# One POOL task a step: scattered stores, running counts and fold sums each tied behind a step's low parts

## The chip, the cores and the metric

The kernel runs on one core of one Trainium2 chip. The metric is the device time of one execution in microseconds, as a median of several runs. A core has five engines that work side by side from queues of their own: TensorE (PE in the profile; matrix products into PSUM), VectorE (DVE), ScalarE (ACT), GpSimd (POOL; elementwise work and indirect DMAs) and SyncE (SP; DMA issue). [...]

## The reference, cut to what matters

```python
X = np.fft.fft(x, axis=1)              # x: 8 x 3072 x 256
X = np.fft.fft(X, axis=2)
x = X.real.reshape(8 * 3072, 256)      # 24576 tokens
h = x @ w_in                           # 256 -> 2048
g = h * np.clip(h + 3.0, 0.0, 6.0) / 6.0
x = g @ w_out                          # 2048 -> 256
expert_idx = np.argmax(x @ w_gate, axis=1)          # one of 8
gate_w = softmax(x @ w_gate)[expert_idx]
out[mask] = gate_w * (np.maximum(x[mask] @ w1[e], 0.0) @ w2[e])   # for each expert e, 256 -> 1024 -> 256
```

## The kernel before, in words

Numbers are carried as two parts, high and low, and a product of two such numbers is three products (high x high, high x low, low x high).

**First stage.** It runs over 8 images (`b`) and, in each, over 6 chunks of 512 tokens (3 groups `g`, 2 halves `c`): 48 chunks in all. A chunk is 8 steps, one for each 256 of the 2048 hidden columns; `step(s)` writes down the instructions of step `s`, so an image is 48 steps and `s % 8` is the place in a chunk. In a step, TensorE multiplies the spectrum `pq` by two blocks of `w_in` into a PSUM tile `ab` (`mm1`; there are two such tiles), and three steps later (`LAG = 3`) the gated result by `w_out` into four accumulators `acc` (`mm2`; 16 matmuls with the high parts `gh`, 8 with the low parts `gl`). Between them, for the step before, VectorE forms `S` and two halves of `h` from `ab` (which frees the tile), ACT forms `r = relu(h/6 + 1/2)`, VectorE the gate product `r <- min(r, 1) * h` (L506, two a step), ACT the high part `gh` and POOL the low part `gl = r - gh` (L183, two a step). `r`, `gh` and `gl` have four buffers each, which is two steps' worth.

After a chunk's last step ACT moves `acc` to SBUF (`xo`) and halves it into `xp`; then `routing` hands out its stages over the following steps through the table `fill`: `s0` and `s1` on VectorE find each token's expert (`rt_oh` is the one-hot choice, L561), `s2` on POOL forms running counts by expert (one copy, then one add of 128x8 for each of four token tiles, L569 and L572), `s3_mm` and `s3` turn them into row numbers `pi` by a small matmul in a tile like `ab`, and `s4(t)` on POOL stores the rows of token tile `t` at scattered places of `xs` by an indirect DMA (`scat`, L148), four a chunk. `s3` comes at `s % 8 = 2` of the next chunk and `s4(0)` to `s4(3)` in the four steps after it.

Beside this, `plan_folds` spreads the preparation of the next image's transform: VectorE's sums over the loaded rows `R` and over `H`, and POOL's four fold sums for each of four quarters (`H <- R`, L180 and L183). It is used for images 1 to 6; image 0 has a plan of its own, and image 7 prepares nothing. `plan_fft` places the transform's own matmuls at fixed steps of an image. `plan_extra` handles one extra row for each image (frequency 128 of the second axis) in image 7, from step `x0 = 7 * 48 + EXTRA`: `parts`, then the matmuls `exbc`, `exa` and `exo` with their VectorE and ACT work (`bc_ev` holds VectorE's outer product) and a low part `exr` on POOL.

**Second stage.** From about 2140 us the scattered rows are read back by expert, and two matrix products run on each tile of rows.

The order in which an engine executes is not that of the source. A scheduler orders each engine's queue from the recorded program; `tc.keep_in_program_order` pins an instruction to the recorded order, and a dependency without a semaphore between two instructions of one engine only says that one comes after the other there.

Of the kernel before, what the change touches and what calls it, by code (L numbers as in the profile page):

```python
# [12 lines left out]
BF16 = mybir.dt.bfloat16  # L13
# [9 lines left out]
P = 128  # L23
# [23 lines left out]
BUFS = dict(h=2, r=4, gh=4, gl=4)  # L47
EXTRA = 23
LATE = (0, 0, 1, 1, 2, 3, 3, 4, 5, 5, 6, 6, 7, 7, 8, 8, 8, 9)
# [25 lines left out]
def tile_fft_moe(ctx, tc, xr, xf, xcoef, w_in, w_out, w_gate, w1, w2, tabs, fm, misc, tri, sgn8, dstc, maskc, out):  # L75
# [69 lines left out]
    dve, act, pool, pe, sp = nc.vector, nc.scalar, nc.gpsimd, nc.tensor, nc.sync  # L145

    def scat(group, **kw):
        i = pool.indirect_dma_start(oob_is_err=False, **kw)  # L148
        tc.declare_no_dep(i.ins, group=group, reason="distinct rows")
        tc.add_to_no_dep_group(group, i.ins)  # L150
# [15 lines left out]
    def pinned(i):  # L166
        if hold.get("fold"):
            tc.keep_in_program_order(i)

    def in_order(f):  # L170
        hold["fold"] = True
        f()
        hold["fold"] = False
# [5 lines left out]
    def add(eng, o, a, b):  # L179
        pinned(eng.tensor_tensor(out=o, in0=a, in1=b, op=ALU.add))  # L180

# [358 lines left out]
    def routing(xo, xp, t0, nt, mask, tagn, wait=RKW):  # L540
# [24 lines left out]

        def s2():
            st["oc"] = oc = sm("rt_oc", [P, 4, NE], BF16)
            oh = st["oh"]
            pool.tensor_copy(oc[:, 0], cnt)  # L569
            for t in range(nt):  # L570
                o = oc[:, t + 1] if t + 1 < nt else cnt
                pool.tensor_tensor(out=o, in0=oc[:, t], in1=oh[:, t], op=ALU.add)  # L572

# [26 lines left out]

        return [("f", s0), ("f", s1), ("f", s2)] + [("f", lambda: None)] * wait + [("p", s3_mm, s3)] + [("f", lambda t=t: s4(t)) for t in range(nt)]

    if True:
# [93 lines left out]
        def plan_folds(b):  # L697
# [6 lines left out]
            for n in range(24, 28):  # L704
                at[n] = max(at[n], FFT_AT[2][1] + 1 + (n - 24) // 2)
            assert at[32] < FFT_AT[0][0] and at[39] < FFT_AT[1][0] + 6 * STEPS
            for o, hf, n in ((oa, 0, 0), (oa, 1, 4), (ob, 0, 8), (ob, 1, 18)):
                fill[u0 + at[n] - AHEAD].insert(0, o[9 * hf])
                for f in o[9 * hf + 5:9 * hf + 9]:
                    fill[u0 + at[n + 3] + 1].append(lambda f=f: in_order(f))  # L710
            for f, n in zip(seq, at):
# [209 lines left out]
        def step(s):  # L921
# [22 lines left out]
            if 0 < s <= NS:  # L944
# [9 lines left out]
                for n in range(2):  # L954
                    sub(pool, gl[n], g[n], gh[n])
                hold[("g", s - 1)] = (gh, gl)
# [319 lines left out]
```

## Time and profile before

| | |
|---|---|
| median of 3 runs | 3331.14 us (3330.49 to 3333.17) |
| the profiled execution's own time | 3328.47 us |
| its span, first to last instruction | 3326.5 us |
| busy: TensorE, VectorE, ACT, POOL | 3061.1, 2603.8, 1808.6, 2290.0 us |
| the `gl` of POOL (L183), 768 | 1128.5 us |
| the gate products of VectorE (L506), 768 | 730.3 us |
| mean granted clock of TensorE | 0.973 of full speed |

The span is shorter than the execution's time by 1.97 us of start and end. The busy times are sums over stages with different limits: the share of an engine in the whole says little on what a stage waits for, so stretches and timelines are read below.

### The profile page before, as it was taken

Reading aid. Unit: us, or ns where it says so; the run is one execution under the profiler, and the core shown is the slowest. Engines: PE = TensorE matmul, PEld = TensorE weight load, DVE = VectorE, ACT = ScalarE, POOL = GpSimd, SP = SyncE. Lnnn points to the kernel's source line nnn. Section 1 sums busy time; section 2 is a strip of 40 time slices with the busy share of each in tenths; the row PEclk is TensorE's granted clock in tenths of the full one; section 3 lists DMA queues with packets and bytes.
Section 4 is the critical chain, followed back from the end, with each engine's and each line's share of the span. In section 5 each row is a group of like instructions: output and inputs, shape, how many; then the busy total and the mean of one; then the engine's idle time right before and its main releaser. Section 6 shows DMA issues by size and latency. Waiting matters only on the chain. (4 is left out here: it accounts for less than half of the span.)

```text
span 3326.5 us, 61143 instructions
## 1 busy us (share of the span) xinstructions
PE 3061.1 (92%) x22747; PEld 2927.8 (88%) x22747; DVE 2603.8 (78%) x4258; ACT 1808.6 (54%) x3020; POOL 2290.0 (69%) x1781
## 2 busy tenths in 40 slices
PE   5888889889999989989989999999999999999998
PEld 5888889889899889989989998888888888898887
DVE  8999999999999998999999997855555555555553
ACT  4556556555555555556556665544454454454453
POOL 5577776876876866876876665666666666666664
PEclk9999999999999999999999999999999999999999
DMA  5110100100100100100000002075555555555560
GB/s 194 39 35 28 38 25 13 40 23 14 43 25 14 42 25 14 37 30 14 33 14 16 14 14 52 21 206 150 145 167 145 144 155 154 148 146 154 148 171 29
DMA packets 246830, 242.77 MB, mean 73 GB/s; under 512 B 148379, under 2 KB 209660, under 8 KB 246528
## 3 DMA queue, kind: packets, MB, share of 16 engines
q1 hardware_dynamic: 225280, 184.33, 19.7%
q0 software_dynamic: 21248, 54.49, 4.5%
q8 instruction: 181, 2.97, 0.4%
q14 instruction: 121, 0.99, 0.1%
HBM read 159.71 MB, written 54.04 MB: 64 GB/s over the span
## 5 line engine op out<-in xcount | busy, mean ns | idle before, releaser
L183 POOL TENSOR_TENSOR gl<-r,gh 128x512 fp32r<-128x512 f32 x768 | 1128.5, 1493 | 461.4 <-ACT gh L953 251.2
L511 PE MATMUL acc<-WO,gh 128*128 128x264 f32 x6144 | 851.6, 293 | 12.7 <-ACT xo L530 11.6
L511 PEld LDWEIGHTS acc<-WO,gh 128*128 128x128 f32 x6144 | 814.0, 198 | 13.9 <-ACT xo L530 12.0
L506 DVE SCALAR_TENSOR_TENSOR r<-r,h 128x512 f32<-128x512 f32 x768 | 730.3, 976 | 51.6 <-ACT r L499 49.4
L953 ACT ACTIVATE gh<-r 128x512 fp32r<-128x512 f32 x768 | 473.7, 630 | 528.7 <-DVE r L506 390.0
L499 ACT ACTIVATE r<-h,half 128x512 f32<-128x512 f32 x768 | 523.9, 720 | 272.6 <-DVE h L183 207.0
L164 PE MATMUL ab<-pq,WA 128*128 128x256 f32 x2304 | 417.7, 291 | 151.0 <-DVE rt_mc L549 72.2
L987 DVE SCALAR_TENSOR_TENSOR WB<-hp,WA 128x512 fp32r<-128x512 f32 (+1 forms) x472 | 278.7, 606 | 304.2 <-ACT WA L986 300.0
L164 PEld LDWEIGHTS ab<-pq,WA 128*128 128x128 f32 x2304 | 337.4, 193 | 161.0 <-issue 137.6
L511 PE MATMUL acc<-WO,gl 128*128 128x264 f32 x3072 | 440.8, 285 | 4.1 <-POOL gl L183 4.1
L164 PE MATMUL ab<-pq,WB 128*128 128x256 f32 x2304 | 414.8, 290 | 0.0
L511 PEld LDWEIGHTS acc<-WO,gl 128*128 128x128 f32 x3072 | 401.1, 189 | 6.3 <-POOL gl L183 6.2
L188 DVE SCALAR_TENSOR_TENSOR S<-pb,w,ab 128x256 f32<-128x256 f32 x768 | 333.9, 472 | 52.1 <-PE ab L164 51.2
L986 ACT ACTIVATE WA<-hp 128x512 fp32r<-128x512 f32 (+1 forms) x472 | 241.4, 531 | 195.5 <-PE hp L164 194.7
L164 PEld LDWEIGHTS ab<-pq,WB 128*128 128x128 f32 x2304 | 342.5, 196 | 0.0
L148 POOL DMA_INDIRECT out_dram<-yo,dst x200 | 217.8, 1089 | 156.0 <-DVE yo L1087 118.5
L164 PE MATMUL hp<-xTb,TB 128*128 128x512 f32 (+1 forms) x1344 | 277.2, 364 | 13.6 <-DVE WB L987 13.6
L164 PE MATMUL op<-W2b,WA 128*128 128x256 f32 x1536 | 277.8, 283 | 0.0
L164 PE MATMUL hp<-xTa,W1b 128*128 128x512 f32 (+1 forms) x1392 | 275.6, 357 | 1.9 <-DVE WB L987 1.9
L164 PEld LDWEIGHTS hp<-xTb,TB 128*128 128x128 f32 x1344 | 225.7, 188 | 57.8 <-DVE WB L987 15.3
L148 POOL DMA_INDIRECT xs_dram<-xp,pic x192 | 215.1, 1120 | 84.8 <-issue 28.4
L1087 DVE TENSOR_SCALAR yo<-op,gd 128x256 f32<-128x256 f32 x200 | 95.4, 478 | 219.6 <-PE op L164 217.8
(268 smaller groups left out, 5208.6 us busy)
## 6 DMA issues: line engine op xcount, KB each, us to landing
w1a<-in_w_dram SPq DMA_DIRECT2D x29, 1024.0 KB, 5.0
w1b<-in_w_dram SPq DMA_DIRECT2D x29, 1024.0 KB, 4.9
w2b<-in_w_dram SPq DMA_DIRECT2D x58, 512.0 KB, 4.0
R<-in_xr_dram SPq DMA_DIRECT2D x32, 774.0 KB, 4.2
w2a<-in_w_dram SPq DMA_DIRECT2D x29, 768.0 KB, 4.9
w2d<-in_w_dram SPq DMA_DIRECT2D x28, 256.0 KB, 4.3
raw<-in_w_in_dram SPq DMA_DIRECT2D x8, 512.0 KB, 4.1
rawo<-in_w_out_dram SPq DMA_DIRECT2D x8, 512.0 KB, 3.4
```

The lines of the kernel that those rows point to most:

```text
L148: i = pool.indirect_dma_start(oob_is_err=False, **kw)
L164: pe.matmul(dst, l, r, start=(n == 0), stop=(n == len(terms) - 1))
L183: i = eng.tensor_tensor(out=o, in0=a, in1=b, op=ALU.subtract)
L188: pinned(dve.scalar_tensor_tensor(out=o, in0=a, scalar=s, in1=b, op0=ALU.mult, op1=ALU.add))
L499: act.activation(r, h, AF.Relu, bias=half, scale=1.0 / 6.0)
L506: dve.scalar_tensor_tensor(out=g, in0=r, scalar=1.0, in1=h, op0=ALU.min, op1=ALU.mult)
L511: pe.matmul(acc[t][:, 0:GW], lhs, wo(w, f0 + i), start=st, stop=sp_)
L953: act.activation(gh[n], g[n], AF.Copy)
L986: act.activation(hi, ps, AF.Relu)
L987: dve.scalar_tensor_tensor(out=lo, in0=ps, scalar=0.0, in1=hi, op0=ALU.max, op1=ALU.subtract)
L1087: dve.tensor_scalar(yo[:, j], ps[:, 0:D], t["gd"][:, j, 0:1], None, op0=ALU.mult)
```

## The change

A helper `behind(i)` is new: it adds an order without a semaphore, so that instruction `i` comes after the latest `gl` that has been recorded (`hold["gl"]`, set in `step`). It is applied to each scattered store into `xs`, to each instruction of the running counts, and in `plan_folds` to POOL's fold sums. `s2` becomes `s2(t)`, one add a step over four steps, where all stood in one step before. The four fold sums of a quarter are put into four steps, one each, in place of one step for all; they are no longer pinned to the recorded order. The extra row starts two steps later (`EXTRA` 25).

```diff
-EXTRA = 23
+EXTRA = 25
...
+    def behind(i):
+        tc.add_manual_dep(i.ins, hold["gl"].ins.name, mybir.DependencyInfo(mybir.DependencyClass.NoSync, mybir.DependencyReason.DATA),
+                          reason="one a step")
+
     def scat(group, **kw):
         i = pool.indirect_dma_start(oob_is_err=False, **kw)
+        if group == "xs":
+            behind(i)
...
     def add(eng, o, a, b):
-        pinned(eng.tensor_tensor(out=o, in0=a, in1=b, op=ALU.add))
+        i = eng.tensor_tensor(out=o, in0=a, in1=b, op=ALU.add)
+        pinned(i)
+        return i
...
-        def s2():
-            st["oc"] = oc = sm("rt_oc", [P, 4, NE], BF16)
-            oh = st["oh"]
-            pool.tensor_copy(oc[:, 0], cnt)
-            for t in range(nt):
-                o = oc[:, t + 1] if t + 1 < nt else cnt
-                pool.tensor_tensor(out=o, in0=oc[:, t], in1=oh[:, t], op=ALU.add)
+
+        def s2(t):
+            if t == 0:
+                st["oc"] = sm("rt_oc", [P, 4, NE], BF16)
+                behind(pool.tensor_copy(st["oc"][:, 0], cnt))
+            oc = st["oc"]
+            o = oc[:, t + 1] if t + 1 < nt else cnt
+            behind(pool.tensor_tensor(out=o, in0=oc[:, t], in1=st["oh"][:, t], op=ALU.add))
...
-        return [("f", s0), ("f", s1), ("f", s2)] + [("f", lambda: None)] * wait + [("p", s3_mm, s3)] + [("f", lambda t=t: s4(t)) for t in range(nt)]
+        return [("f", s0), ("f", s1)] + [("f", lambda t=t: s2(t) if t < nt else None) for t in range(wait + 1)] + [("p", s3_mm, s3)] + [("f", lambda t=t: s4(t)) for t in range(nt)]
...
-                for f in o[9 * hf + 5:9 * hf + 9]:
-                    fill[u0 + at[n + 3] + 1].append(lambda f=f: in_order(f))
+                for k, f in enumerate(o[9 * hf + 5:9 * hf + 9]):
+                    fill[u0 + at[n + 3] + 1 + k].append(lambda f=f: behind(f()))
...
                 for n in range(2):
-                    sub(pool, gl[n], g[n], gh[n])
+                    hold["gl"] = sub(pool, gl[n], g[n], gh[n])
```

On POOL, at the end of a chunk of image 4 that has no fold sums near it (steps 218 to 222), the queue of the kernel before reads so; the number behind `gl` is the step that recorded it, and `x3` is three instructions alike:

```order
L183 TENSOR_TENSOR gl218_0_15747<-r218_0_15743,gh218_0_15745 128x512
L183 TENSOR_TENSOR gl218_1_15748<-r218_1_15744,gh218_1_15746 128x512
L569 COPY rt_occ26_15975<-cnt_63 128x8
L148 DMA xs_dram<-xp207_15196,pic25_15767 198656x260 x3
L572 TENSOR_TENSOR rt_occ26_15975<-rt_occ26_15975,rt_ohc26_15910 128x8
L148 DMA xs_dram<-xp207_15196,pic25_15767 198656x260
L572 TENSOR_TENSOR rt_occ26_15975<-rt_occ26_15975,rt_ohc26_15910 128x8 x2
L572 TENSOR_TENSOR cnt_63<-rt_occ26_15975,rt_ohc26_15910 128x8
L183 TENSOR_TENSOR gl219_0_15824<-r219_0_15820,gh219_0_15822 128x512
L183 TENSOR_TENSOR gl219_1_15825<-r219_1_15821,gh219_1_15823 128x512
```

The changed kernel's queue at the same place, on the same engine:

```order
L192 TENSOR_TENSOR gl219_1_15825<-r219_1_15821,gh219_1_15823 128x512
L153 DMA xs_dram<-xp207_15193,pic25_15767 198656x260
L192 TENSOR_TENSOR gl220_0_15892<-r220_0_15888,gh220_0_15890 128x512
L192 TENSOR_TENSOR gl220_1_15893<-r220_1_15889,gh220_1_15891 128x512
L153 DMA xs_dram<-xp207_15193,pic25_15767 198656x260
L192 TENSOR_TENSOR gl221_0_15960<-r221_0_15956,gh221_0_15958 128x512
L192 TENSOR_TENSOR gl221_1_15961<-r221_1_15957,gh221_1_15959 128x512
L153 DMA xs_dram<-xp207_15193,pic25_15767 198656x260
L579 COPY rt_occ26_15975<-cnt_63 128x8
L582 TENSOR_TENSOR rt_occ26_15975<-rt_occ26_15975,rt_ohc26_15910 128x8
L192 TENSOR_TENSOR gl222_0_16026<-r222_0_16022,gh222_0_16024 128x512
L192 TENSOR_TENSOR gl222_1_16027<-r222_1_16023,gh222_1_16025 128x512
```

Nothing stands between the low parts of steps 218 and 219 any more; the stores follow one behind each pair from step 219 on, and the copy and the adds one behind each from step 221 on.

Where POOL's fold sums are near (image 4, steps 196 to 198), the queue before reads on POOL:

```order
L572 TENSOR_TENSOR rt_occ23_14339<-rt_occ23_14339,rt_ohc23_14251 128x8 x3
L572 TENSOR_TENSOR cnt_63<-rt_occ23_14339,rt_ohc23_14251 128x8
L183 TENSOR_TENSOR gl197_0_14315<-r197_0_14311,gh197_0_14313 128x512
L183 TENSOR_TENSOR gl197_1_14316<-r197_1_14312,gh197_1_14314 128x512
L180 TENSOR_TENSOR H5_1_13552<-R5_1_0_13550 128x2x129
L183 TENSOR_TENSOR H5_1_13552<-R5_1_0_13550 128x2x129
L183 TENSOR_TENSOR H5_1_13552<-R5_1_0_13550 128x129
L180 TENSOR_TENSOR H5_1_13552<-R5_1_0_13550 128x129
L183 TENSOR_TENSOR gl198_0_14393<-r198_0_14389,gh198_0_14391 128x512
```

And in the changed kernel:

```order
L192 TENSOR_TENSOR gl197_1_14316<-r197_1_14312,gh197_1_14314 128x512
L187 TENSOR_TENSOR H5_1_13552<-R5_1_0_13550 128x2x129
L153 DMA xs_dram<-xp183_13543,pic22_14107 198656x260
L579 COPY rt_occ23_14336<-cnt_63 128x8
L582 TENSOR_TENSOR rt_occ23_14336<-rt_occ23_14336,rt_ohc23_14251 128x8
L192 TENSOR_TENSOR gl198_0_14387<-r198_0_14383,gh198_0_14385 128x512
L192 TENSOR_TENSOR gl198_1_14388<-r198_1_14384,gh198_1_14386 128x512
L192 TENSOR_TENSOR H5_1_13552<-R5_1_0_13550 128x2x129
L153 DMA xs_dram<-xp183_13543,pic22_14107 198656x260
L582 TENSOR_TENSOR rt_occ23_14336<-rt_occ23_14336,rt_ohc23_14251 128x8
L192 TENSOR_TENSOR gl199_0_14451<-r199_0_14447,gh199_0_14449 128x512
```

One fold sum, one store and one add now stand between two steps' low parts, in several steps on end, where four fold sums stood in a row.

Around the extra row (image 7), POOL's queue before:

```order
L183 TENSOR_TENSOR gl362_1_25716<-r362_1_25712,gh362_1_25714 128x512
L148 DMA xs_dram<-xp351_25115,pic43_25735 198656x260 x4
L183 TENSOR_TENSOR gl363_0_25799<-r363_0_25795,gh363_0_25797 128x512
L183 TENSOR_TENSOR gl363_1_25800<-r363_1_25796,gh363_1_25798 128x512
L183 TENSOR_TENSOR exr_25422<-exf_25423,exr_25422 128x128
```

And in the changed kernel:

```order
L192 TENSOR_TENSOR gl364_0_25873<-r364_0_25869,gh364_0_25871 128x512
L192 TENSOR_TENSOR gl364_1_25874<-r364_1_25870,gh364_1_25872 128x512
L153 DMA xs_dram<-xp351_25115,pic43_25684 198656x260
L192 TENSOR_TENSOR exr_25540<-exf_25541,exr_25540 128x128
L192 TENSOR_TENSOR gl365_0_25945<-r365_0_25941,gh365_0_25943 128x512
```

The low part `exr` now follows one store and the low parts of step 364, where it followed four stores and those of step 363.

## Rows read from the trace of the kernel before

**Rows 1.** Windows, us busy (x instructions) by engine, TensorE's granted clock, DMA share, GB/s

```profile
300.00:2000.00 1700.00, 1552.31 (x12314) 1529.40 (x12313) 1589.97 (x2657) 1002.29 (x1768) 1258.24 (x1104) 0.96 0.07 25
```

**Rows 2.** Groups, 300 to 2000 us: count, busy us, mean ns, idle before and releasers

```profile
L506 DVE SCALAR_TENSOR_TENSOR r<-r,h 128x512 f32<-128x512 f32 x642 | 605.0, 968 | 47.1 <-ACT r L499 44.9
...
L164 PE MATMUL ab<-pq,WA 128*128 128x256 f32 x1920 | 346.4, 290 | 133.0 <-DVE rt_mc L549 72.2 <-DVE xp L591 28.5 <-DVE rt_sc L590 24.0
...
L561 DVE SCALAR_TENSOR_TENSOR rt_ohc<-rt_ixc,iom 128x32 bf16<-128x32 f32 x40 | 26.7, 667 | 0.0
```

**Rows 3.** Timeline of TensorE, 1250 to 1275 us: start, length, instruction, idle before

```profile
1258.96 0.59 PE L164 MATMUL ab<-pq,WA 128*128 128x256 f32 x3 [2.64 <-DVE rt_mc L549]
...
1260.84 3.26 PE L511 MATMUL acc<-WO,gh 128*128 128x264 f32 x16
...
1264.90 0.52 PE L164 MATMUL ab<-pq,WA 128*128 128x256 f32 x3
...
1266.34 2.10 PE L511 MATMUL acc<-WO,gh 128*128 128x264 f32 x16
...
1269.26 0.52 PE L164 MATMUL ab<-pq,WA 128*128 128x256 f32 x3
```

**Rows 4.** Timeline of POOL, 1256.5 to 1290 us

```profile
1256.90 2.51 POOL L183 TENSOR_TENSOR gl<-r,gh 128x512 fp32r<-128x512 f32 x2 [1.79 <-ACT gh L953]
...
1261.40 0.98 POOL L148 DMA_INDIRECT xs_dram<-xp,pic  x1 [0.30 <-issue]
...
1262.69 1.42 POOL L148 DMA_INDIRECT xs_dram<-xp,pic  x1 [0.30 <-DVE r L506]
...
1266.41 6.23 POOL L183 TENSOR_TENSOR gl<-r,gh 128x512 fp32r<-128x512 f32 x4
...
1283.13 3.00 POOL L183 TENSOR_TENSOR gl<-r,gh 128x512 fp32r<-128x512 f32 x2 [1.79 <-ACT gh L953]
```

**Rows 5.** Timeline of VectorE, 1256.5 to 1290 us

```profile
1258.14 0.68 DVE L180 TENSOR_TENSOR h<-S,ab 128x512 f32<-128x512 f32 x1
...
1261.97 1.29 DVE L506 SCALAR_TENSOR_TENSOR r<-r,h 128x512 f32<-128x512 f32 x2
...
1267.33 2.62 DVE L506 SCALAR_TENSOR_TENSOR r<-r,h 128x512 f32<-128x512 f32 x2
...
1271.40 1.78 DVE L506 SCALAR_TENSOR_TENSOR r<-r,h 128x512 f32<-128x512 f32 x1
...
1283.64 1.33 DVE L180 TENSOR_TENSOR H<-H 128x516 f32<-128x516 f32 x1
```

**Rows 6.** Timeline of ACT, 1260 to 1266 us

```profile
1263.65 1.15 ACT L953 ACTIVATE gh<-r 128x512 fp32r<-128x512 f32 x2 [1.27 <-PE acc L511]
```

**Rows 7.** Timeline of ACT, 1142 to 1150 us

```profile
1145.82 0.72 ACT L499 ACTIVATE r<-h,half 128x512 f32<-128x512 f32 x1 [1.48 <-POOL gl L183]
```

**Rows 8.** Timeline of VectorE, 1152 to 1165 us

```profile
1158.18 3.19 DVE L506 SCALAR_TENSOR_TENSOR r<-r,h 128x512 f32<-128x512 f32 x2 [0.25 <-ACT r L499]
```

**Rows 9.** Timeline of VectorE, 1226 to 1238 us

```profile
1227.02 0.18 DVE L557 SCALAR_TENSOR_TENSOR rt_kc<-rt_dc,iom 128x32 f32<-128x32 f32 x1
...
1228.45 3.06 DVE L561 SCALAR_TENSOR_TENSOR rt_ohc<-rt_ixc,iom 128x32 bf16<-128x32 f32 x1
```

**Rows 10.** Timeline of TensorE, 1226 to 1238 us

```profile
1233.85 0.59 PE L164 MATMUL ab<-pq,WA 128*128 128x256 f32 x3 [2.94 <-DVE xp L591]
```

**Rows 11.** Timeline of POOL, 1343 to 1386 us

```profile
1361.13 13.67 POOL L183 TENSOR_TENSOR gl<-r,gh 128x512 fp32r<-128x512 f32 x8
```

**Rows 12.** Groups of POOL with shapes kept apart, 300 to 2000 us

```profile
L180 POOL TENSOR_TENSOR H<-R 128x258 f32<-128x258 f32 x24 | 25.4, 1057 | 0.0
```

**Rows 13.** Timeline of TensorE, 2004 to 2042 us

```profile
2029.92 7.91 PE L164 MATMUL exo<-WO,exr 128*8 128x264 f32 x46 [4.29 <-POOL exr L183]
```

**Rows 14.** Timeline of POOL, 2017 to 2033 us

```profile
2028.95 0.92 POOL L183 TENSOR_TENSOR exr<-exf,exr 128x128 fp32r<-128x128 f32 x1
```

**Rows 15.** Waits of ACT, 300 to 2000 us: total, times, longest

```profile
ACT r L499 <- POOL gl L183: 36.9, 44, 1.5
```

More of the change, by code (lines that the diff above doesn't have):

```diff
@@ L705, in plan_folds @@
                 at[n] = max(at[n], FFT_AT[2][1] + 1 + (n - 24) // 2)
+            assert at[7] + 4 <= at[12] and at[21] + 4 <= at[28]
             assert at[32] < FFT_AT[0][0] and at[39] < FFT_AT[1][0] + 6 * STEPS
```

## Prediction

> **What bounds the kernel now.** I read the windows first. From 300 to 2000 us, where the Fourier stage and the first expert layer run, VectorE is busy 1590 of 1700 us and TensorE 1552 [rows 1]. So two engines are nearly full, and the question is who makes whom wait. The groups of that stretch answer it: TensorE idles 133 us, all of it ahead of the first matmul of a step, for VectorE to free the PSUM tile `ab`; the names in its row are of whatever VectorE finished last [rows 2]. The same group view shows why VectorE is full. Its gate product (L506, two a step) takes 968 ns on average [rows 2], but 1.29 us for a pair, 0.65 each, where nothing disturbs it [rows 5]. 640 of them at 0.32 us too much are about 205 us.
>
> The timelines of steps 218 to 224 show how the two belong together. TensorE does a step in 4.36 us (1264.90 to 1269.26) until a chunk ends; there the routing takes one of the two `ab` tiles, TensorE waits 2.64 us until VectorE has read the last one (1258.14 + 0.68, and 0.14 later TensorE starts), and the next 16 matmuls take 3.26 us in place of 2.10 [rows 3, 5]. So a chunk lasts as long as VectorE needs from the moment it falls behind to the chunk's end, and only what shortens VectorE there shortens the program.
>
> VectorE's long products stand beside POOL's low parts. The product at 1271.40 takes 1.78 us while `gl` runs [rows 5, 4]: an elementwise POOL operation and a VectorE operation with two inputs in SBUF take turns, each for a whole instruction. A scatter on POOL doesn't do that: the pair at 1261.97 ran beside two scatters in 1.29 us [rows 5, 4].
>
> In steady steps the two engines miss each other: POOL is idle 1.79 us before its pair of `gl` [rows 4], and there VectorE's pair of products fits. What breaks this is the burst after a chunk's end: copy, four scatters and four adds stand on POOL ahead of `gl219`. ACT has the first half of `gh` ready at about 1264.2 [rows 6], POOL starts its four `gl` at 1266.41, 2.1 us late [rows 4], and the next two products of VectorE cost 2.62 us as a pair, the one after them 1.78 [rows 5].
>
> **The change, part by part.** No instruction is added or removed. TensorE's and ACT's orders change around the extra row alone; VectorE's there and by a swap or two an image. POOL's changes throughout, in all chunks; SP's not at all. The expert stage after 2140 us keeps its order.
>
> *Scatters and adds.* `gl219` can start when `gh` is there, 1264.3, and both halves, at 1.25 each [rows 4], are over by 1266.9, before the pair at 1267.33: 1.33 us less on VectorE. The product at 1271.40 may keep its wait (0) or lose it (1.1). The scatters now fill the idle 1.79 us of four later steps. A scatter with its 0.30 us of issue takes 1.3 alone and 1.7 beside products (0.98 and 1.42) [rows 4], so it fits; the copy and an add are some 0.6 more (between the second scatter's end, 1262.69 + 1.42, and 1266.41 [rows 4] stand one scatter of about 1.0 and the four adds, so 0.3 each), and in that step POOL comes 1.7 + 0.6 - 1.79 = 0.5 us late, a little less in the next. Nothing is queued behind on POOL but that step's `gl`, for which VectorE's fold operation waits already (1.33 us at 1283.64 [rows 5]). I give back 0.7 us a chunk for this, and take 1.0 us net, from bounds of 0 and 2.4.
>
> Per image (six chunks) the kinds of chunk differ. Three have a burst alone: two at 1.0, and 0 for the one where a Fourier piece on TensorE lets VectorE catch up in mid-chunk: 2.0. One has four fold sums on POOL shortly before the burst: there the one-hot comparison of 128x32 took 3.06 us while the late `gl` pair ran, and TensorE waited 2.94 us behind it [rows 9, 10]. Undisturbed I put this operation at about 0.2, from the 0.18 us of one of its size [rows 9]; 667 ns is its mean [rows 2]. With `gl` on time it meets at most a fold sum (1.06 [rows 12]): 2.0 less, from bounds of 0 and 2.9. One has fold sums right behind the burst: ACT waited 1.48 us for a buffer of `r` that a late `gl` still read, and a pair of products cost 3.19 instead of 1.29 [rows 7, 8]. Of these 3.4 I take 2.0; below, 0. In the last kind POOL runs eight `gl` without a pause in 13.67 us, 1.71 each where 1.25 would do [rows 11], and fold sums behind them: POOL is full, and spreading full work moves nothing: 0, between -1 and +1. The sum is 6.0 us an image. Six images (1 to 6) are of this kind: 36 us. Image 0 keeps its fold sums in place and image 7 has none; for them I count nothing.
>
> The running counts are read by the routing matmul two or more steps after their last add, and the scattered rows' buffer is wanted again a chunk later; I cost both waits at nothing. If the cover failed, TensorE would wait for a 0.2 us add.
>
> *The extra row, two steps later.* Its low part `exr` now stood behind four scatters and a `gl` pair, ending at 2029.87; TensorE waited 4.29 us for it, and its 46 matmuls then took 7.91 us [rows 13, 14]. In the new order one scatter stands ahead of it, and the chunk's end with its ACT work lies before, not between. The wait goes wholly or to a third, and some of the slow matmuls with it: 5 us, from bounds of 0 and 6.2 (46 at the 0.13 us that 16 in 2.10 [rows 3] make would be 6.0; 4.3 + 1.9).
>
> Sum: 36 + 5 = 41 us. The profiled execution took 3328.47 us; the median shown is 2.67 above, 3331.14. So 3287.5 by the profile, and **3290 us** as a median.
>
> **The rivals.**
> (a) *The phases lock again.* After the burst VectorE and POOL need some four steps to fall back into the steady pattern, and its step with a fold operation (1.79 + 3.00 = 4.79 us [rows 4]) is slower than TensorE's 4.36 whatever came before. Then VectorE reaches the chunk's end hardly earlier: 0.3 us a chunk over 36 chunks, and the extra row: 15 us, 3316. For it: the pattern pulls itself together. Against it: the chunks with fold sums don't reach the pattern in today's trace before they end.
> (b) *More than that.* With shorter waits at the borders the matmuls behind them run in 2.10 in place of 3.26 us, which I have not counted. At the upper bounds alone (3.4 + 2.9 + three at 2.4 + 1 = 14.5 an image, 87 for six, 6.2 for the extra row): 93 us, 3238. Against it: every bound must hold at once.
> (c) *Slower: POOL falls behind for good.* Eight steps an image now hold a fold sum (1.06), a scatter with its issue (1.7), partly a copy and an add (0.6), and the `gl` pair (3.0 [rows 4]): 5.8 to 6.4 us against TensorE's 4.36. Three in a row put POOL 4 to 5 us behind; where that uses up the two steps of slack, ACT waits for `r`, as it does now 44 times for 36.9 us [rows 15]. It decides if that wait comes at three places an image: 1.5 us there and 1.3 of a slowed pair, 50 us over six images, with none of the gain: 3376; with half of it, 3358. For it: the row of eight `gl`. Against it: the same work stands there today in larger lumps.
> (d) *Slower: scatters wait for VectorE's products.* If a scatter beside a pair of products waited out its 1.29 us [rows 5] in place of the 0.44 seen (1.42 less 0.98 [rows 4]), it would take 0.85 more and `gl` come 0.5 us late in four steps of 36 chunks: 72 us back, 3362. The 1.42 speaks against it; it is counted with (c). [...]
> (e) *Nothing*: what a chunk gains in its first steps TensorE's own pace takes: 3331.
>
> **How the numbers follow.** What can be told from no change here is about 0.2%, 6.7 us. Forecast (3265 to 3312): 0.50. (a), 3312 to 3324: 0.15. (b), below 3265: 0.10. (e), within 6.7 us: 0.10. (c) and (d), slower: 0.15. So faster 0.75, same 0.10, slower 0.15. The range runs from the middle of (b), 3250, to the upper side of (e) and the mildest of (c), 3336; outside it I leave 0.07 below and 0.12 above. The forecast's own range is 3265 to 3312.
>
> **What would show it.** Right: after a chunk's end no four scatters in a row on POOL, `gl` within 0.5 us of its `gh`; L506 below 900 ns; the one-hot comparison below 450 ns; ACT's waits for `gl` under 20 us; TensorE's idle time ahead of `ab` between 90 and 110 us in that stretch; no 4.29 us before `exo`. If L506 keeps its 968 ns, (a) or (e). If ACT's waits for `gl` grow past 60 us, (c); scatters of 2 us and more as a rule, (d). The forecast fails if POOL's lateness is not removed but only handed from one step to the next, so that products meet `gl` as often as before.

## The result, and the profile after

The changed kernel takes 3362.68 us (3349.44 to 3369.66, 7 runs) against 3331.12 of the kernel before (7 runs): a ratio of 1.0087 (1.0066 to 1.0108): 31.6 us slower, where 41 us faster was forecast. The profiled execution took 3366.02 us with a span of 3364.2. Within the seven runs the time goes with the mean granted clock of TensorE (3369.66 us at 0.967, 3349.44 at 0.975). The clock alone is not the difference: in the kernel before, run beside the first experiments below, 0.967 goes with 3342.14 us and 0.974 with 3327.08, so at like clock some 22 to 28 us are left (if chips do not differ by as much). Whether the clock is cause or consequence of the rest is not shown. In what follows a *store* is a scatter, one of the 192 indirect DMAs from POOL into `xs`.

The windows and the groups from 300 to 2000 us answer to [rows 1, 2] (the lines moved: L515 is the gate product, L192 the low part, L570 the one-hot choice, L171 `mm1`):

```profile
300.00:2000.00 1700.00, 1528.98 (x12047) 1504.76 (x12046) 1594.52 (x2600) 979.91 (x1729) 1220.69 (x1085) 0.96 0.07 24
```

```profile
L515 DVE SCALAR_TENSOR_TENSOR r<-r,h 128x512 f32<-128x512 f32 x628 | 562.6, 924 | 33.7 <-ACT r L508 32.3
...
L197 DVE SCALAR_TENSOR_TENSOR R<-R 128x516 f32<-128x516 f32 (+1 forms) x47 | 84.2, 1792 | 0.0
L187 DVE TENSOR_TENSOR R<-R 128x516 f32<-128x516 f32 (+1 forms) x47 | 71.9, 1529 | 0.0
L187 DVE TENSOR_TENSOR H<-H 128x516 f32<-128x516 f32 (+1 forms) x36 | 63.2, 1755 | 0.0
...
L570 DVE SCALAR_TENSOR_TENSOR rt_ohc<-rt_ixc,iom 128x32 bf16<-128x32 f32 x39 | 7.1, 182 | 0.0
...
L171 PE MATMUL ab<-pq,WA 128*128 128x256 f32 x1881 | 343.9, 293 | 154.7 <-DVE rt_mc L558 71.8 <-DVE xp L601 37.5 <-DVE h L187 24.4
```

What was forecast for single operations largely came: the gate products fell from 968 to 924 ns, the one-hot choice from 667 to 182. But VectorE is as busy as before and the program gets less far in the stretch. VectorE's fold operations became slower. The same groups of the kernel before:

```profile
L180 DVE TENSOR_TENSOR R<-R 128x516 f32<-128x516 f32 (+1 forms) x47 | 50.9, 1082 | 0.0
L188 DVE SCALAR_TENSOR_TENSOR R<-R 128x516 f32<-128x516 f32 (+1 forms) x47 | 49.7, 1058 | 0.0
L180 DVE TENSOR_TENSOR H<-H 128x516 f32<-128x516 f32 (+1 forms) x36 | 41.3, 1148 | 0.0
```

These three rows alone hold 77 us more (84.2 + 71.9 + 63.2 less 50.9 + 49.7 + 41.3). The timelines of POOL and of VectorE in chunk kind "POOL is full" (image 4) show one of the slow ones:

```profile
1384.14 1.26 POOL L153 DMA_INDIRECT xs_dram<-xp,pic  x1 [0.15 <-PE acc L520]
1385.41 2.56 POOL L192 TENSOR_TENSOR gl<-r,gh 128x512 fp32r<-128x512 f32 x2
1387.92 1.39 POOL L192 TENSOR_TENSOR H<-R 128x258 f32<-128x258 f32 x1
```

```profile
1385.65 3.15 DVE L197 SCALAR_TENSOR_TENSOR R<-R 128x774 f32<-128x774 f32 x1
```

The fold operation comes 0.24 us after the first `gl` has begun. By the prediction it gets its turn at that one's end, some 1 us later, as in [rows 4, 5], where a pair of `gl` with a fold operation between them takes 3.00 us. Here the two `gl` run in 2.56 us without a break and VectorE waits for both. What stands out is that this pair begins right at the end of a store (1384.14 + 1.26); whether that is the reason the experiments have to show.

To count this, each VectorE operation's time above the shortest one of its kind (same operands and shape) was summed over the first stage (from the first low part to the last), by what stood on POOL while it waited: one elementwise operation; two or more that follow a store without a gap (under 60 ns from each to the next; one add of the counts may stand first); two or more elsewhere. These sums are worked out from all instructions of the traces, in us, with the number of operations. They move by up to some 15 us with the limits chosen, the differences between the rows by less:

```
                 stage   one POOL op    2+ behind a store   2+ elsewhere   sum
before            2090   347.7 (518)     49.2 (18)            4.0 ( 4)     401
changed           2124   322.1 (499)    106.1 (51)           11.4 (13)     440
stores            2088   320.6 (483)    100.5 (50)            2.3 ( 2)     424
untied            2130   321.4 (504)    109.6 (34)            9.6 (12)     441
untiedpad         2066   335.0 (549)      0                  27.7 (22)     363
beforepad         2078   343.6 (525)      2.3 ( 2)           17.2 (10)     364
```

The forecast gain is there: 26 us less of waits behind one operation. Against it stand 57 us more behind stores and 7 elsewhere: 39 us more on VectorE, 34 us more of stage. A sum of waits is not yet time, though: the row `stores`, an experiment below, has as much behind stores as the changed kernel and the stage of the kernel before.

### The profile page after: what moved, and what is told of

It reads as the page before. It is cut to its first block, busy times and chain, and to the rows that moved or that the text cites. A ratio compares the mean times of both kernels' runs of the same rounds, so it can differ in the third digit from the quotient of the medians.

```text
span 3364.2 us, 61099 instructions
## 1 busy us (share of the span) xinstructions
PE 3076.3 (91%) x22747; PEld 2943.2 (87%) x22747; DVE 2638.3 (78%) x4258; ACT 1806.9 (54%) x3020; POOL 2285.3 (68%) x1781
## 3 DMA queue, kind: packets, MB, share of 16 engines
q8 instruction: 181, 2.97, 0.4%
## 5 line engine op out<-in xcount | busy, mean ns | idle before, releaser
L192 POOL TENSOR_TENSOR gl<-r,gh 128x512 fp32r<-128x512 f32 x768 | 1076.3, 1422 | 570.2 <-PE acc L520 278.8
L515 DVE SCALAR_TENSOR_TENSOR r<-r,h 128x512 f32<-128x512 f32 x768 | 692.6, 928 | 43.4 <-ACT r L508 41.9
L171 PE MATMUL ab<-pq,WA 128*128 128x256 f32 x2304 | 424.0, 294 | 173.8 <-DVE rt_mc L558 71.8
L171 PEld LDWEIGHTS ab<-pq,WA 128*128 128x128 f32 x2304 | 342.0, 196 | 187.4 <-issue 169.6
L171 PE MATMUL ab<-pq,WB 128*128 128x256 f32 x2304 | 418.2, 292 | 0.0
L171 PEld LDWEIGHTS ab<-pq,WB 128*128 128x128 f32 x2304 | 345.9, 199 | 0.0
L171 PE MATMUL hp<-xTb,TB 128*128 128x512 f32 (+1 forms) x1344 | 277.2, 364 | 13.6 <-DVE WB L998 13.6
L171 PE MATMUL op<-W2b,WA 128*128 128x256 f32 x1536 | 277.9, 283 | 0.0
L171 PE MATMUL hp<-xTa,W1b 128*128 128x512 f32 (+1 forms) x1392 | 275.6, 357 | 1.2 <-DVE WB L998 1.2
L171 PEld LDWEIGHTS hp<-xTb,TB 128*128 128x128 f32 x1344 | 225.9, 188 | 57.6 <-DVE WB L998 15.2
L171 PEld LDWEIGHTS hp<-xTa,W1b 128*128 128x128 f32 x1392 | 227.9, 188 | 41.8 <-DVE WB L998 1.6
```

What stands on the lines that cost most here:

```text
L171: pe.matmul(dst, l, r, start=(n == 0), stop=(n == len(terms) - 1))
L192: i = eng.tensor_tensor(out=o, in0=a, in1=b, op=ALU.subtract)
L515: dve.scalar_tensor_tensor(out=g, in0=r, scalar=1.0, in1=h, op0=ALU.min, op1=ALU.mult)
```

## The experiments

Ratios are to the kernel before, run on the same chip in turn, with 95% intervals. The kernel before took 3331.1 to 3341.5 us from chip to chip (medians), so runs of different chips are compared by their ratios.

**First four: which part, and spacers.** Theories: T1, a VectorE operation loses its turn where two low parts follow a store without a gap (51 operations of the changed kernel, 18 of the kernel before, by the table above; the expectations, which count up to 2000 us and with other limits, have 56 and 16); T2, POOL has too much in each step (rival c); T3, a phase that happens to be bad.

`pads2`: the changed kernel with

```diff
+        if group == "xs":
+            for n in range(2):
+                p = pool.tensor_copy(pad[:, 0:8], pad[:, 8:16])
+                after_of(p, i)
+                i = p
+            hold["pad"] = i
...
```

> The changed kernel with two 128x8 copies on POOL (onto scratch that nobody reads) right behind each of its 192 scattered stores and ahead of the next low part. Three theories stand for the 31.5 us that the change cost. [...] By T1 the copies stand in the place of the pair: losses under 10, VectorE's fold operations (R and H, 256 us for 160 in images 1 to 6, 171 before) back under 190 us, and the time at 3300 to 3330. T2, POOL is late because every step now holds something (rival c of the prediction): 0.4 us more a store makes it worse, 3365 to 3400. T3, the fold operations merely stand at a phase where the pair runs, whatever is ahead of it: losses stay above 40, 3355 to 3375.

3342.23 us, 1.0015 (0.9998 to 1.0032). Waits behind a store fell from 106 to 21 us, and the ratio by 0.7 per cent, less than T1 had forecast: waits behind one operation rose from 322 to 379, with 192 times two copies more on POOL. The ranges of T2 and T3 were missed, so neither is the whole of it.

`lumpfold`, `foldspread`: the fold sums undone, and alone.

```diff
-                for k, f in enumerate(o[9 * hf + 5:9 * hf + 9]):
-                    fill[u0 + at[n + 3] + 1 + k].append(lambda f=f: behind(f()))
+                for f in o[9 * hf + 5:9 * hf + 9]:
+                    fill[u0 + at[n + 3] + 1].append(lambda f=f: in_order(f))
```

> The changed kernel with the four fold sums of a quarter in one lump on POOL again; stores and counts stay one a step. T1 (turn lost behind a store): the stores still stand right ahead of `gl` in busy chunks, so losses stay at 35 or more and the time at 3345 to 3370. T2 (a fold sum in each step overloads POOL): back to 3310 to 3335.

3342.61, 1.0017 (1.0004 to 1.0030): between the two ranges, and below T1's though 89 us of waits behind stores were left.

> The kernel before with its POOL fold sums one a step, each behind that step's low parts; stores, counts and extra row as before. T1: only the burst's last store can stand right ahead of `gl`, so 16 losses or so as before, VectorE's fold operations under 190 us, 3315 to 3335. T2 (a fold sum in each step makes POOL late): 3345 and more.

3330.58, 0.9985 (0.9974 to 0.9996): the fold sums alone cost nothing, so T2 is out for them alone.

`extra25`: the kernel before with `EXTRA = 25`.

> The kernel before with the extra row two steps later and nothing else. The prediction's term of 5 us (bounds 0 and 6.2) gives 3326; a wait that only moves gives 3331.

3330.38, 0.9984 (0.9970 to 0.9999): some 5 us (0.3 to 10), the term of the prediction.

**Next four: other places for the store, and the two engines by themselves.** `mid` puts each store between the two `gl` of the next step, `midlump` also has lumps of fold sums, `scatfirst` puts the store ahead of the fold sum of its step. In the cut from `mid`, `f()` records the store.

```diff
                 for n in range(2):
                     hold["gl"] = sub(pool, gl[n], g[n], gh[n])
+                    if n == 1 and "sc" in hold:
+                        after_of(hold["gl"], hold.pop("sc"))
+                    for f in hold.pop("late", []) if n == 0 else []:
+                        f()
...
```

> The changed kernel with each scattered store between the two `gl` of a step (images 0 to 6) in place of behind the pair; POOL's instructions and their number are the same. T1 (the turn is lost where two low parts follow a store without a gap): only one `gl` now follows a store, and VectorE has the store's own 1 us for itself, so losses of a whole pair under 10, VectorE's fold operations of images 1 to 6 under 200 us (256 in the changed kernel), 3310 to 3340. T2 (POOL has too much in each step): its load is the same, 3350 to 3370.

3388.11, 1.0158 (1.0134 to 1.0182): a miss for both theories. The second `gl` comes a store later, waits behind one operation rise by some 50 us, and over 80 us stay behind stores, now with a fold sum or an add as the second operation.

> The same as the run before it, stores between the two `gl`, and the fold sums of a quarter in one lump again. T1: the some 48 losses of the run with lumps alone (3342.6) go: 3310 to 3335. T2: POOL's load is that of the run with lumps alone, so 3335 to 3350.

3391.52, 1.0162 (1.0138 to 1.0185): the same.

> The changed kernel with one thing turned round: in a step that holds a store and a fold sum, the store comes first, and the fold sum and the add stand between it and the next `gl`. T1: where a fold sum stands there, the pair keeps its handover; where the store is alone, it is lost as before: losses of a whole pair from 56 to some 30, 3340 to 3358. T2: the same work in each step, 3355 to 3370.

3345.93, 1.0023 (1.0010 to 1.0037): the time fell in T1's range, but not for its reason, since some 100 us behind stores stayed. What makes it 0.6 per cent faster than the changed kernel is open.

`byitself`: nothing of the kernel but 480 VectorE additions in a row and a list of POOL work.

```python
    v(60)
    many(12, lambda: gl(2))
    v(60)
    many(8, scat, lambda: gl(2))
    v(60)
    many(8, scat, lambda: gl(4))
    v(60)
    many(8, scat, lambda: copy(1), lambda: gl(2))
    v(60)
    many(8, scat, lambda: copy(2), lambda: gl(2))
...
```

> Not the kernel's work: only POOL and VectorE, and the output is filled with constants. VectorE runs 480 additions of 128x512 in a row; POOL runs 24 subtractions of 128x512, then, eight times each, a scattered store with two subtractions, a store with four, a store with one, two and three 128x8 copies and two subtractions, and a plain DMA from its queue with two. T1: without a store they take turns, an addition in each gap (POOL 1.25 to 1.9 us a subtraction, VectorE some 1.9); behind a store the first two POOL operations run in a row and one addition takes some 3.1 us; with one copy a copy and a subtraction are the two (some 2.1), with two or three copies no loss beyond 1.9; with four subtractions only the first two run in a row. T3: turns throughout, no addition over 2 us. What a plain DMA does is open.

No addition took over 2.2 us, near what T3 has: behind a store VectorE got its turn after the first subtraction. T1 as it stood was not shown outside the kernel.

**The factors one by one.** A new theory, T4: the stores had stood in a hole of POOL.

`untied` takes the tie off the stores, `untiedlump` also undoes the fold sums, `stores` has nothing but the tied stores.

```diff
         i = pool.indirect_dma_start(oob_is_err=False, **kw)
-        if group == "xs":
-            behind(i)
```

> The changed kernel without the tie on the scattered stores alone: they stand again ahead of a chunk's first `gl`, four in a row, while counts and fold sums stay one a step and the extra row late. T4, a new theory: POOL stood idle ahead of that `gl` for some 5.5 us in many chunks, since TensorE and ACT were not yet there; the four stores (4 x 1.3 us) lay in this hole, and the tie moved them into steps that have none, so POOL's idle time ahead of `gl` rose from 353 to 448 us between 300 and 2000 us. By T4 the stores alone cost what was lost and the counts gave a gain: 3300 to 3325. T1 (turns lost behind a store): losses fall from 56 to some 16 to 36, 3315 to 3335. T2 (the sums and counts in every step overload POOL): stays at 3345 and more.

3367.99, 1.0103 (1.0086 to 1.0119): in T2's range, far from those of T4 and T1.

> As the run before it, with the fold sums in lumps too: only the counts one a step, and the late extra row. T4: 3300 to 3325, the counts being what made `gl` late in the kernel before. If the counts are nothing, 3326, the extra row's 5 us alone.

3378.63, 1.0133 (1.0117 to 1.0150): both ranges missed.

> The kernel before with the tie on the scattered stores alone; counts, fold sums and extra row as before. T4 and T1: the whole loss or more, 3350 to 3375, POOL's idle time ahead of `gl` over 420 us from 300 to 2000 us. T2: near the kernel before, 3325 to 3340.

3327.99, 0.9984 (0.9975 to 0.9994): in T2's range, and T1's and T4's were missed. T4 is false, stores tied one a step are no loss. T1 is missed in an instructive way: VectorE did lose its turns, 100 us of them behind stores, and it cost no time. What all slow variants share is the moved *counts*. In the kernel before a copy and four adds stood between the stores and the next `gl`; moved one a step, they leave a store right ahead of it.

`phases`: by themselves again, with additions at all phases.

> Not the kernel's work: only POOL and VectorE, the output filled with constants. VectorE runs an addition with both inputs in SBUF, then one to three with one input in PSUM, of several lengths, so that its two-input additions come at all phases of POOL's work; POOL runs, 24 times each, two subtractions of 128x512 behind one 128x8 copy, behind a scattered store, behind a store and two copies, and behind a plain DMA. T1: an addition that starts inside the first subtraction gets its turn ahead of the second (1.9 us or less from the start of the first) but for the second group, where it waits for both (its end over 2.5 us after the start of the first); a saturated VectorE did not show it, since its addition stood there before the first subtraction. If T1 is wrong, no group differs.

No group differed: a VectorE addition that starts in the first subtraction ends 1.80 to 1.86 us after that one's start, behind a store too (three that start late in it, behind copies, 2.32). By this T1 was wrong, or the kernel had something more.

**What stands behind the last store.** `untiedpad` is `untied` with two copies behind the fourth store of a chunk, in the old place of the counts, and no others.

```diff
+            for n in range(2 if hold.get("lastst") else 0):
+                p = pool.tensor_copy(pad[:, 0:8], pad[:, 8:16])
...
+            hold["lastst"] = t == nt - 1
...
```

> The changed kernel with the stores untied (3368), and two 128x8 copies on POOL, onto scratch that nobody reads, behind the last of a chunk's four stores alone, ahead of the next low part. In the kernel before, the copy and the adds of the counts stood in that place. T1 (a `gl` right behind a store denies VectorE its turns): VectorE's time lost to two and more POOL operations right behind a store falls from 110 us to under 45, and the time to 3325 to 3345. T5, the rival: the counts cost where they now stand, one in each of four steps: no change, 3360 to 3375.

3305.86, 0.9913 (0.9894 to 0.9933): 62 us (1.9 per cent) faster than `untied` by 96 copies of some 0.3 us, and faster than both kernels. That is below T1's range even; T5 is out. Timelines of POOL and VectorE at the same chunk end (steps 218 and 219, image 4), `untied` first:

```profile
1283.59 1.23 POOL L153 DMA_INDIRECT xs_dram<-xp,pic  x1 [0.30 <-issue]
1284.82 2.56 POOL L190 TENSOR_TENSOR gl<-r,gh 128x512 fp32r<-128x512 f32 x2
```

```profile
1285.35 3.19 DVE L513 SCALAR_TENSOR_TENSOR r<-r,h 128x512 f32<-128x512 f32 x2
```

and `untiedpad`:

```profile
1254.97 0.97 POOL L159 DMA_INDIRECT xs_dram<-xp,pic  x1 [0.30 <-issue]
1255.94 0.66 POOL L164 COPY pad<-pad 128x8 bf16<-128x8 bf16 x2
1256.57 2.52 POOL L202 TENSOR_TENSOR gl<-r,gh 128x512 fp32r<-128x512 f32 x2
```

```profile
1258.35 1.89 DVE L525 SCALAR_TENSOR_TENSOR r<-r,h 128x512 f32<-128x512 f32 x2
```

The pair of products costs 1.89 in place of 3.19 us. These rows show more than a turn given back: in `untied` the products start 0.53 us into the pair of `gl` and wait for both, in `untiedpad` 1.78 us into it and wait for the second alone, and there too the pair runs without a break. So part of what the copies bring is that fewer operations meet the pair at all: of the 47 pairs behind them 38 met none that had to wait for their first `gl`, 8 gave the turn. How the 62 us divide between the two is not shown. Some ten steps on, where stores stand between low parts, `untied` has its worst: three `gl` run in a row behind a store, and one product waits for all of them.

```profile
1331.86 3.80 POOL L190 TENSOR_TENSOR gl<-r,gh 128x512 fp32r<-128x512 f32 x3
```

```profile
1331.71 4.50 DVE L513 SCALAR_TENSOR_TENSOR r<-r,h 128x512 f32<-128x512 f32 x1
```

`waits`: as `phases`, but each subtraction takes an input copied for it by ACT, so it waits on a semaphore.

```diff
-            keep(pool.tensor_tensor(out=go, in0=ga, in1=gb, op=ALU.subtract))
...
+            act.activation(hh, gb, AF.Copy)
+            keep(pool.tensor_tensor(out=oo, in0=ga, in1=hh, op=ALU.subtract))
```

> Not the kernel's work: POOL and VectorE by themselves as in the run with all phases, but each subtraction now takes an input that ACT copies for it and waits for it by a semaphore, as `gl` waits for `gh`, with four buffers. Groups of 24: two subtractions behind one copy, behind a store, behind a store and two memsets, behind a store and two copies. T1 needs something that the earlier runs by themselves lacked; if that is the semaphore, additions that start inside the first subtraction end over 2.5 us after its start in the second group and by 1.9 us in the others. If no group differs, the loss in the kernel hangs on more than a store and a wait.

Now the loss is there outside the kernel. Behind a store all 24 additions ended 3.05 to 3.06 us after the first subtraction's start; behind two memsets or two copies the same code gives 1.80 to 1.81 (33 of 37; of those that start late in the first, three ended at 2.3 and one at 3.5; behind one copy without a store one of 13 ended at 2.8). The run has ACT's copies and four buffers beside the semaphores; that it is the semaphores among these is the likeliest reading, but not shown apart. POOL's timeline in the group with a store, and in that with memsets:

```profile
150.98 2.49 POOL L117 TENSOR_TENSOR oo<-ga,hh 128x512 f32<-128x512 f32 x2
153.63 1.26 POOL L133 DMA_INDIRECT xs<-xp,pi  x1 [0.17 <-issue]
154.92 2.49 POOL L117 TENSOR_TENSOR oo<-ga,hh 128x512 f32<-128x512 f32 x2
...
191.02 0.99 POOL L133 DMA_INDIRECT xs<-xp,pi  x1 [0.16 <-issue]
192.02 0.28 POOL L122 MEMSET pad<- 128x8 bf16 x2
192.26 2.94 POOL L117 TENSOR_TENSOR oo<-ga,hh 128x512 f32<-128x512 f32 x2
```

VectorE's additions beside these two (150.98 and 192.26):

```profile
150.99 3.03 DVE L107 TENSOR_TENSOR vo<-va,vb 128x512 f32<-128x512 f32 x1
...
192.43 1.64 DVE L107 TENSOR_TENSOR vo<-va,vb 128x512 f32<-128x512 f32 x1
```

and in the run without semaphores, behind a store:

```profile
101.06 1.26 POOL L124 DMA_INDIRECT xs<-xp,pi  x1 [0.16 <-issue]
102.34 2.97 POOL L113 TENSOR_TENSOR go<-ga,gb 128x512 f32<-128x512 f32 x2
```

2.49 us is two subtractions back to back, 2.94 and 2.97 two with an addition between them.

`nocounts` is the changed kernel with the counts as before; `nocountspad` has two memsets behind each store.

> The changed kernel with the counts alone as before: copy and four adds in one lump, not tied; stores and fold sums one a step, the extra row late. If the parts add up (stores, fold sums and extra row 0.16, 0.15 and 0.16 per cent faster each when alone): 3310 to 3325. If stores and fold sums in the same steps overload POOL (T2): 3335 and more.

3336.65, 1.0007 (0.9993 to 1.0022): without the move of the counts the slowdown is gone, but the three small gains don't add up, and the time is in T2's range. The waits behind stores are not gone: some 100 us, as in the changed kernel.

> The same, with two 128x8 memsets on POOL behind each store. T1: the 100 us that VectorE lost behind stores in the run with tied stores alone fall under 40, 3295 to 3315, if a memset stands in for a copy; if not, as the run before it or some 5 us more.

3335.44, 1.0004 (0.9994 to 1.0015), above T1's range. These two runs differ by the memsets alone and show the turn itself most plainly, and that getting it back need not be worth any time. In `nocounts` 47 `gl` pairs began within 30 ns of a store's end while a VectorE operation waited, and none let it in between; behind the memsets 114 pairs met a waiting operation, and all 114 let it in. One place in both, first `nocounts`:

```profile
1286.70 1.26 POOL L153 DMA_INDIRECT xs_dram<-xp,pic  x1 [0.16 <-issue]
1287.95 2.57 POOL L192 TENSOR_TENSOR gl<-r,gh 128x512 fp32r<-128x512 f32 x2
```

```profile
1288.40 2.42 DVE L184 SCALAR_TENSOR_TENSOR SS0s<-H,SS0s 128x254 fp32r<-128x254 f32 x1
```

and `nocountspad`:

```profile
1292.78 0.30 POOL L166 MEMSET pad<- 128x8 bf16 x2
1293.08 2.72 POOL L204 TENSOR_TENSOR gl<-r,gh 128x512 fp32r<-128x512 f32 x2
```

```profile
1293.23 1.41 DVE L196 SCALAR_TENSOR_TENSOR SS0s<-H,SS0s 128x254 fp32r<-128x254 f32 x1
```

Yet the time is the same: waits behind stores all but went, those behind one operation rose to some 380 us. One store a step with spacers trades one for the other.

**What the counts' move is worth by itself.** `beforepad` is the kernel before with two memsets behind each store, `untiedpadall` is `untied` with the same.

> The kernel before with two 128x8 memsets on POOL behind each store (they take 0.12 us each where measured by themselves). It too lost VectorE's turns behind a store, 18 times, 49 us in all, where no add happened to stand between. If the 26 us of the run with stores untied and copies behind the last store are only these losses cured: 3300 to 3312 here too. If the counts' move, one a step, is a gain by itself, as the prediction had it: some of the 26 us only, 3312 to 3328.

3317.80, 0.9933 (0.9912 to 0.9955). The kernel before took 3341.53 us on this chip, some 10 more than the two ranges were set from; by the ratio, the gain of 0.67 per cent (22 us) is most of the 26 and speaks for the first.

This trace also holds what the runs with a plain DMA by themselves could not show. POOL's queue loads a small table (`sgn`) by a plain DMA once an image, and in six images a `gl` pair follows it within 22 ns, with no memset between. VectorE's operation that needs 0.41 us took 2.52 to 2.90 there, all six times (13 us in all):

```profile
466.04 0.60 POOL L275 DMA_DIRECT2D sgn<-in_sgn_dram  x1
466.66 2.54 POOL L195 TENSOR_TENSOR gl<-r,gh 128x512 fp32r<-128x512 f32 x2
```

```profile
466.96 2.53 DVE L189 SCALAR_TENSOR_TENSOR SC<-H,SC 128x254 fp32r<-128x254 f32 x1
```

> The changed kernel with the stores untied and two 128x8 memsets behind each store in place of two copies behind the last of four. T1: no loss behind a store is left, also not where a store stands between two low parts (6 in the run with copies behind the last): 3295 to 3308. If memsets between the stores lengthen the lump more than they save: 3308 to 3315.

3312.77, 0.9916 (0.9895 to 0.9937). Both intervals hold the other's middle: of the gain of `untiedpad` most is what `beforepad` has too, with the kernel before's own 49 us behind stores cured. Run side by side the two differ by 5 us (3312.11 to 3313.91 against 3316.68 to 3319.93). That is what the move of counts and sums and the late extra row add together, and the extra row's own 5 us would fill it. The six losses that the expectation puts behind stores stand behind `sgn`, and are still here.

## Why the prediction was wrong

*What bounds the kernel*: right in the main. The sum of VectorE's waits beside POOL (401 to 440 us) moved with the stage (2090 to 2124), and the two shortest stages of the table have the two smallest sums. It is not the sum alone: `stores` has 424 us and a stage of 2088, so where a wait falls counts too.

*The step that failed* is the sentence that "an elementwise POOL operation and a VectorE operation with two inputs in SBUF take turns, each for a whole instruction". It holds elsewhere (518 of 540 waiting operations of the kernel before waited for one POOL operation alone), but right behind a store the low parts run on uninterrupted and VectorE waits for both (`waits`: 3.05 us against 1.81; `nocounts` against `nocountspad`: 47 of 47 turns lost, 114 of 114 given). The trace of before had it in plain sight: the one-hot choice of [rows 9] needs some 0.2 us and took 3.06, more than one `gl` (1.25) can explain. These are the rows of POOL there:

```profile
1227.77 1.13 POOL L148 DMA_INDIRECT xs_dram<-xp,pic  x1 [0.30 <-issue]
1228.92 2.53 POOL L183 TENSOR_TENSOR gl<-r,gh 128x512 fp32r<-128x512 f32 x2
```

I read the 3.06 as the price of a late pair and counted on winning it back by coming in time. It was the price of a store right ahead of the pair, and the change puts 51 waits of that kind where 18 were. In `waits` VectorE's addition waited for a whole subtraction at the least (1.81 us, of which the subtraction is 1.26); behind a store POOL's second subtraction also ran ahead of it (3.05 us). Where the inputs lie matters in `waits`: from 70 to 174 us, mostly behind stores, additions with both in SBUF took 2609 ns on average, from 186 to 297 us, mostly behind memsets, 1045; those with one input in PSUM took 547 and 546.

*How much of the 31.6 us this is* is shown in part. Two copies behind each store took 0.72 of the 0.87 per cent back (`pads2`). But `stores` and `nocounts` carry the same waits behind stores, some 100 us, and were not slower than the kernel before. What such a wait costs depends on where it falls: 49 us of them cured were worth 22 us to the kernel before (`beforepad`), 100 us cured were worth nothing to `nocounts`. Why, no run shows.

*Scatters and adds*: 1.0 us a chunk net. The gross side was about right: 26 us of waits behind one operation, and 17 us by which the one-hot choices fell over images 1 to 6, which had stood behind stores, are 43; the forecast's 36 and its give-back, 0.7 us for two chunks in each of six images, are 44. The give-back was the mis-sized term: 57 + 7 us, and those 17 that other waits behind stores took the place of, are 81 us, or 1.7 us over each of 48 chunks. Counting the copy and the adds as a burden alone (0.6 us) missed that they kept a store and a low part apart; putting two copies into their old place is worth most (`untied` against `untiedpad`, 62 us).

*Chunk kinds*: I gave the "POOL is full" kind 0; from step 43 to 50 of an image it went from 41.3 to 44.5 us (mean of images 1 to 6), the largest loss.

*The extra row*: 5 us forecast, 0.16 per cent (0.01 to 0.30) measured alone, which is 5 us. Its wait of 4.29 us is gone:

```profile
2072.47 5.95 PE L171 MATMUL exo<-WO,exr 128*8 128x264 f32 x48
```

*Indicators*: low parts earlier, right in the main (in images 1 to 6 none of 288 pairs begins over 2 us after its `gh`, 82 did before; the mark of 0.5 us is still missed by 109, before by 144); ACT's waits for `gl` gone from the list; the one-hot choice under 450 ns. Wrong: gate products under 900 ns (924), TensorE's idle time 90 to 110 us (154.7). The prediction's own sign of failing, products that meet `gl` as often as before, nearly came: 499 waits behind one operation, 518 before. That mix said where to look: what was moved came earlier, something else paid.

*The rivals*: (d) gave 3362, which the time happens to be, by luck: its mechanism is another. It has stores wait for products, and they do not show the 2 us that it asked for as a rule (1242 ns on average, 1134 before). (c) needed late low parts and ACT waiting for them; neither came.

Open are why two low parts run on uninterrupted behind a store, and whether it is their semaphore waits that count, why the lost turns cost time in some variants and not in others, and why the fold sums cost 0.7 per cent beside tied counts and stores (the changed kernel against `lumpfold`) and nothing alone. For the last two T2, too much on POOL in each step, is not ruled out as a part.

## What to carry to other kernels

A small instruction may be worth its place for what it separates: before moving work off a queue, read what will then stand side by side. Where an operation takes longer than the one it waits for can explain, find the second one; such a row is a mechanism not yet in the sum. Here two 128x8 memsets on POOL behind each indirect store, ahead of elementwise work that waits on a semaphore, made the kernel before 0.67 per cent faster, and `untied` 1.9 per cent; with one store a step (`nocounts`) they gave the turns back and no time. So a lost turn is worth finding, and its price has to be measured.

## What the runs showed of the hardware

- Behind an indirect DMA on POOL's queue two subtractions that wait on semaphores ran back to back in `waits` (2.49 us), and a VectorE operation with two inputs in SBUF got its turn only after both (3.05 against 1.81 us); in `untied` three low parts in a row were seen too (3.80, VectorE 4.50). In `stores`, of the pairs that began within 30 ns of a store's end with a VectorE operation waiting, 48 of 49 gave it no turn in between; of 57 with 121 ns or more of idle time in front, at most one was lost.
- A plain DMA on that queue did the same: behind the load `sgn` six of six in `beforepad` (2.52 to 2.90 us for an operation of 0.41).
- One 128x8 add in between did not help 27 pairs of the changed kernel (store's end to `gl` mostly 169 to 192 ns): they were lost all the same. So it is not the time since the store alone.
- Two small operations in between gave the turn back, 128x8 memsets (0.28 us for two, also beside a busy VectorE) 114 of 114 times in `nocountspad`, and these or 128x8 copies (0.2 us each undisturbed) 33 of 37 times in `waits`.
- By themselves and without semaphores on POOL's operations, in `phases`, the effect was not there (1.84 us behind a store, and as much behind a plain DMA). The run with semaphores, `waits`, has ACT's copies beside it too.
